# One branch block, forward and backward: stores issued by GpSimd, Z transposed with a later query tile, the last merge transposed by TensorE, x summed in place

## The chip, the cores and the metric

The kernel runs on one core of one Trainium2 chip. The metric is the device time of one execution in microseconds (us), as the median over several runs. TensorE (PE) multiplies, VectorE (DVE), ScalarE (ACT) and GpSimd (POOL) work on its results, and SyncE (SP) does nothing but issue DMAs here: plain copies and DMA transposes.

## The reference

```python
B, T, D, K = 2, 4000, 144, 5                    # all bf16
xa = layernorm(x)
q, k, v = split(xa @ w_qkv)                     # D columns each
p = softmax(q @ k.T * D ** -0.5)                # 4000 x 4000 per batch
glob = (p @ v) @ w_att_out
h = gelu(xa @ w_mlp_in); u, g = split(h)
gc = depthwise_conv(layernorm(g), dw_csgu)      # 5 taps over tokens
loc = (u * gc) @ w_mlp_out
m = concat(glob, loc)
m = m + depthwise_conv(m, dw_merge)             # 5 taps over tokens
out = x + m @ w_merge
...
_out, _vjp = jax.vjp(_f, x, w_qkv, ..., w_merge)
return out, *_vjp(grad_out)                     # out, dx and seven weight gradients
```

## The kernel before

The 4000 tokens of a batch are 32 blocks of 125 rows (`PB`), 64 query tiles for the two batches. Four stages follow each other: a head (loads, layernorms, the weights multiplied together), the attention (`phase_att`, 65 steps, tile i's work spread over several steps), the merge (class `Merge`) and the weight gradients (class `Final`), whose pieces lie between those of the merge.

**A step of the attention.** TensorE makes four pairs of chunks, scores of tile s and dP of tile s-1, each of 1000 columns (128 rows of the contraction in L1181, the 16 left over in L1188). DVE negates a chunk of scores to `Pbuf` and takes its minimum (L1203), ACT exponentiates (L1209) and copies dP to `Sbuf` (L1219), DVE multiplies the two (L1220). SP transposes halves of `Pbuf` and `Sbuf` by DMA to `PT` (L1213) and `ST` (L1408). From these TensorE makes Y (L1230) and Z (L1269), both into one PSUM tile `yz`, of which there is one buffer. Of Y, ACT makes `yn` (L1243, two buffers; stored to `Yn_d`) and three products, and POOL adds two of them to `QBs` (L1252, five buffers). Of Z, DVE makes `zn` (L1273, two buffers; stored to `Zn_d`), which a DMA transpose of its own turns into `zt` (L1281). `X_group` (L1325) sums dS and P against `QBs`, and `zt` against a product of weights, into `acc`. The next query tile, laid out in `qb` of 512 columns, is turned into `qt` by a DMA transpose (L1162).

**Beside it** run the units of the local branch (`local_units`): a group of two blocks passes gelu, layernorm, five taps and their backward; its product `ug` is stored to `ug_d` (L658). Batch 1's layernorm and products (`prep_late`) start at step 27.

**The merge** reads `Yn_d`, `ug_d` and `Zn_d` back (`Yg`, `Zn`), makes transposed copies `goT` and `YT` of 36 blocks, and multiplies them with prepared weights: `out_g` (16 groups of four blocks) forms `po` in PSUM (L1717, L1719), DVE adds it to the loaded `xo` (five buffers) into a tile `o_` (two buffers, L1720), and SP stores `o_`. `dx_a` and `dx_b` make the other output, `dxo`, whose last sum POOL does (L1746) and SP stores. The two batches get their transposed copies in two ways: batch 0 by 72 TensorE transposes and ACT copies (`transposes`, L1529 and L1530), batch 1 by `turn`: POOL copies four blocks to `ym` (L1671, three buffers) and SP issues a DMA transpose (L1672).

**What sets the order.** A `Planner` holds a table of numbers (`ORDER`), one permutation for each engine, and chains the instructions of each engine in that order. Each engine, SP and POOL too, does its list strictly in order: an instruction that waits holds all behind it. `move` (L47, L48) copies 125 rows as 112 and 13. Each DMA also signals one of eight semaphores of its queue in rotation, and waits for the DMA that used that semaphore before it.

Of the kernel before, what the change touches and what calls it, by code (L numbers as in the profile page):

```python
# [8 lines left out]
BF = mybir.dt.bfloat16  # L9
# [6 lines left out]
D = 144  # L16
DR = 16
# [98 lines left out]
class Head:  # L116
# [7 lines left out]
    def loads(self):  # L124
# [287 lines left out]
def prep_late(k, W, b, S, es, pst):  # L412
# [85 lines left out]
    def xar(g):  # L498
# [4 lines left out]
        for c in (2 * g, 2 * g + 1):  # L503
            nc.sync.dma_start(S.XR[32 * (c % 4):32 * (c % 4) + DR, (c // 4) * CH:(c // 4 + 1) * CH], S.R[96:112, c * CH:(c + 1) * CH])
# [17 lines left out]
def local_units(k, W, b, S, A, es, DHT, ps_w, gw):  # L522
# [10 lines left out]
    nc.sync.dma_start(held[1][PB - 1:PB].rearrange("p a b c -> p (a b c)"), k.zdram[0:1, 0:4 * D])  # L533
# [81 lines left out]
    def e_dgc(g):  # L615
# [37 lines left out]
    def gc_unit(g):  # L653
# [4 lines left out]
        nc.sync.dma_start(S.ug_d[:, G2 * g:G2 * g + G2, :], ug[:])  # L658
# [113 lines left out]
class Planner:  # L772

    ORDER = {
# [322 lines left out]
def phase_att(k, W, SS, A, head, E0, E1, prep, hooks):  # L1097
# [30 lines left out]
    def clr():  # L1128
        for t_ in qbr:
            nc.gpsimd.memset(t_[:], 0.0)  # L1130
# [1076 lines left out]
```

## Time and profile before

| | us |
|---|---|
| median of three runs | 1181.19 (1180.3 to 1187.23) |
| profiled execution | 1190.94 |
| its span | 1189.2, granted clock 0.992 |
| busy PE | 1134.5 (95% of the span) |
| busy DVE | 1021.0 (86%) |
| busy ACT | 913.0 (77%) |
| busy POOL | 228.1 (19%) |
| share of the DMA engines' span taken by the hardware queue | 81.4% |

The profiled execution is one single execution, some ten us above the median of the runs beside it; a sum made from its rows is set against its own time. The span runs from the first to the last instruction. Busy times of different engines overlap. The DMA row is the time of the packets on the 16 DMA engines as a share of 16 times the span.

### The profile page before, as it was taken

What the parts mean: (1) busy time and instruction counts of PE and PEld (TensorE: products, weight loads), DVE (VectorE), ACT (ScalarE), POOL (GpSimd) and SP (SyncE); (2) the same over time, 40 slices, a digit from 0 to 9 for tenths busy, and PEclk for the clock granted to TensorE, in tenths of its full rate; (3) what the DMA queues carried; (4) which work ended last, traced back from release to release, by engine and by line L of the source; (5) the groups of instructions that cost most, each with busy time, mean ns of one, the idle gap of its engine ahead of it and who ended that gap; (6) DMA issues with size and microseconds to landing.
All of it is one profiled execution on the core that took longest, in us unless ns stands there. A gap on an engine that the chain in (4) does not pass through costs nothing. (4 is left out here: it accounts for less than half of the span.)

```text
span 1189.2 us, 36104 instructions
## 1 busy us (share of the span) xinstructions
PE 1134.5 (95%) x14389; PEld 880.8 (74%) x14389; DVE 1021.0 (86%) x3043; ACT 913.0 (77%) x1662; POOL 228.1 (19%) x383
## 2 busy tenths in 40 slices
PE   6999999999999889999999999999999999998898
PEld 3667777777777667777676777777777776898887
DVE  8579999999999989778799999999999985676555
ACT  5999888888998766678898888888889766453252
POOL 7111112111112123200011111111111020023441
PEclk9999999999999999999999999999999999999989
DMA  3778888899898999778998988878989889857643
GB/s 106 165 167 167 160 165 176 177 159 182 167 185 165 166 172 203 167 149 170 205 193 160 160 171 161 185 157 172 167 175 165 174 167 181 205 148 185 157 124 97
DMA packets 673144, 198.43 MB, mean 167 GB/s; under 512 B 648915, under 2 KB 666889, under 8 KB 672955
## 3 DMA queue, kind: packets, MB, share of 16 engines
q1 hardware_dynamic: 671846, 194.74, 81.4%
q8 instruction: 112, 1.84, 0.7%
q0 software_dynamic: 592, 1.18, 0.4%
q14 instruction: 56, 0.46, 0.1%
q10 hardware_dynamic: 538, 0.21, 0.1%
HBM read 24.45 MB, written 17.85 MB: 36 GB/s over the span
## 5 line engine op out<-in xcount | busy, mean ns | idle before, releaser
L1203 DVE TENSOR_SCALAR_CACHE_REDUCE Pbuf<-ps 125x1000 bf16<-125x1000 f32 x256 | 306.3, 1197 | 47.0 <-PE ps L1188 37.5
L1219 ACT CAST Sbuf<-ps 125x1000 bf16<-125x1000 f32 x252 | 252.3, 1001 | 101.5 <-PE ps L1188 81.7
L1209 ACT ACTIVATE Pbuf<-Pbuf,nm 125x1000 bf16<-125x1000 bf16 x256 | 284.9, 1148 | 7.7 <-DVE nm L1205 7.4
L1325 PE MATMUL X<-QBs,Sbuf 125*128 125x144 bf16 x2048 | 282.8, 226 | 0.8 <-ACT QBs L1248 0.4
L1325 PE MATMUL X<-QBs,Pbuf 125*128 125x144 bf16 x2048 | 281.5, 226 | 1.0 <-POOL QBs L1252 0.6
L1181 PE MATMUL ps<-xaT_m,qt 128*128 128x500 bf16 x1024 | 262.3, 376 | 6.7 <-DVE Pbuf L1203 4.9
L1325 PEld LDWEIGHTS <-Sbuf 125*128 125x128 bf16 x2048 | 198.4, 98 | 18.7 <-issue 18.3
L1325 PEld LDWEIGHTS <-Pbuf 125*128 125x128 bf16 x2048 | 200.1, 98 | 2.1 <-issue 1.6
L1220 DVE TENSOR_TENSOR Sbuf<-Sbuf,Pbuf 125x1024 bf16<-125x1024 bf16 x252 | 172.0, 687 | 8.0 <-ACT Pbuf L1209 5.4
L1230 PE MATMUL yz<-xa_aug,PT 125*128 125x145 bf16 x2048 | 151.1, 228 | 14.1 <-DMA PT<-Pbuf 13.2
L1269 PE MATMUL yz<-xa_aug,ST 125*128 125x144 bf16 x2048 | 151.4, 229 | 4.9 <-DMA ST<-Sbuf 4.6
L1230 PEld LDWEIGHTS <-PT 125*128 125x128 bf16 x2048 | 131.7, 98 | 29.4 <-DMA PT<-Pbuf 18.7
L1181 PEld LDWEIGHTS <-qt 128*128 128x128 bf16 x1024 | 92.0, 98 | 70.6 <-issue 9.6
L1269 PEld LDWEIGHTS <-ST 125*128 125x128 bf16 x2048 | 133.2, 98 | 14.7 <-issue 8.0
L1252 POOL TENSOR_TENSOR QBs<-g,g 125x144 bf16<-125x144 f32 x64 | 35.7, 558 | 451.1 <-ACT g L1251 293.9
L1332 DVE TENSOR_TENSOR acc<-X,acc 125x432 f32<-125x432 f32 (+1 forms) x204 | 110.1, 547 | 13.7 <-PE X L1325 13.0
L1188 PEld LDWEIGHTS <-qt 16*128 16x128 bf16 x1024 | 26.4, 91 | 110.2 <-issue 110.2
L1188 PE MATMUL ps<-XR,qt 16*128 16x500 bf16 x1016 | 100.4, 380 | 0.0
L1744 ACT ACTIVATE t<-t,dx_c,rstd_x 125x144 f32<-125x144 f32 x64 | 28.6, 500 | 50.7 <-DVE t L1743 45.6
L649 DVE TENSOR_TENSOR l_prod<-ring,Wc 125x720 bf16<-125x720 bf16 x128 | 66.0, 535 | 0.2
L677 POOL TENSOR_SCALAR l_w<-ring,nc,c 125x144 f32<-125x144 bf16 x64 | 30.7, 485 | 176.1 <-DVE nc L673 86.1
L1614 PE MATMUL Hps<-Yg,go_h 125*128 125x144 bf16 x640 | 55.9, 229 | 1.5 <-DMA Yg<-ug_d 1.5
(558 smaller groups left out, 1941.7 us busy)
## 6 DMA issues: line engine op xcount, KB each, us to landing
Yn_d<-yn SPq DMA_DIRECT2D x64, 35.2 KB
Zn_d<-zn SPq DMA_DIRECT2D x64, 35.2 KB
ug_d<-ugr SPq DMA_DIRECT2D x32, 70.3 KB
PT<-Pbuf SPq DMA_TRANSPOSE x126
ST<-Sbuf SPq DMA_TRANSPOSE x126
acc_d<-acc SPq DMA_DIRECT2D x4, 504.0 KB
go_h<-in_grad_out_dram SPq DMA_DIRECT2D x8, 252.0 KB
Yg<-ug_d SPq DMA_DIRECT2D x8, 252.0 KB
```

What stands on the lines that cost most here:

```text
L649: nc.vector.tensor_tensor(prod[:, bi].rearrange("p a b -> p (a b)"), ring[:, a, p + bi:p + bi + 5, :].rearrange("p a b -> p (a b)"), W.Wc[ ...
L1181: mm = nc.tensor.matmul(pp[r // 2][:, r % 2, 0:CH], QT[i][:, 2 * h, :], bs(i)[0].xaT_m[:, c * CH:(c + 1) * CH], start=True, stop=False)
L1188: nc.tensor.matmul(pp[r // 2][:, r % 2, 0:CH], QT[i][rs, 2 * h + 1, :], xr, start=False, stop=True)
L1203: nc.vector.tensor_scalar(pv(pc(i, c2)), src, -1.0, 3.0e38, op0=ALU.mult, op1=ALU.min, accum_out=NM[i][:, c2:c2 + 1])
L1209: nc.scalar.activation(v, v, ACT.Exp, bias=NM[i][:, 4:5], scale=-1.0)
L1219: nc.scalar.copy(pv(sc(i, c2)), src)
L1220: nc.vector.tensor_tensor(sc(i, c2), sc(i, c2), pc(i, c2), op=ALU.mult)
L1230: nc.tensor.matmul(Yw, PT[0:PB, pos(i, j), :], S.xa_aug[:, j, 0:D + 1], start=(j == 0), stop=(j == NB - 1))
L1269: nc.tensor.matmul(Zw, ST[0:PB, j, :], S.xa_aug[:, j, 0:D], start=(j == 0), stop=(j == NB - 1))
L1325: nc.tensor.matmul(X[:, jj, :], l, r, start=(n_ == 0), stop=(n_ == len(ops) - 1))
L1332: nc.vector.tensor_tensor(av, X[0:PB, 0:nj, :], av, op=ALU.add)
L1614: nc.tensor.matmul(H[0:rows, a // 3, (a % 3) * D:(a % 3 + 1) * D], lhs, self.src[b][h][:, 2 + j, :], start=(n == 0 and a % 3 == 0), stop=( ...
```

## The change

Six things are changed together.

1. **Stores by GpSimd.** The stores of `yn` (64), `zn` (64), `ug` (32), `dxo` (32 DMAs) and of batch 0's `xa` (32 DMAs before, 16 after) go from SP's queue to POOL's, with twelve small copies and fills of `prep_late` and `local_units`.
2. **Z with a later query.** `zn` no longer has a tile of its own: it lies in columns 512 to 767 of the query tile `qb`, and the transpose of query tile i turns six blocks in place of four, the last two of them Z of tile i-4. Sixty of the 62 transposes of `zt` are gone, and `qt` has five buffers.
3. **The last merge by TensorE.** `turn` and `ym` are gone: 18 POOL copies and 18 DMA transposes. Batch 1 uses `transposes`, as batch 0 does: 72 TensorE transposes and ten ACT copies.
4. **x summed in place.** `o_` is gone; DVE adds `po` into `xo`, which is stored. `xo` has nine buffers in place of five.
5. **Small things.** Five loads of weights in the head go from ACT's queue to SP's; copies of 125 or 124 rows between `ring`, `held` and `keep` are cut into 112 rows and the rest; nine fills with zeros become two; three columns of statistics share one tile.
6. **A new table** for all five engines. The change's title says that its order was found with the eight DMA semaphores.

```diff
@@ in several places: another queue
-        nc.sync.dma_start(S.Yn_d[:, j0, :], yn[:])
+        nc.gpsimd.dma_start(S.Yn_d[:, j0, :], yn[:])
-        nc.sync.dma_start(S.Zn_d[:, i % NB, :], zn[0:PB, 0:D])
+        nc.gpsimd.dma_start(S.Zn_d[:, i % NB, :], zn[0:PB, 0:D])
-        nc.sync.dma_start(S.ug_d[:, G2 * g:G2 * g + G2, :], ug[:])
+        nc.gpsimd.dma_start(S.ug_d[:, G2 * g:G2 * g + G2, :], ug[:])
-    k.spill_xa0 = lambda j: move(nc.sync, k.xa_d[:, j:j + 2, :], SS[0].xa_aug[:, j:j + 2, 0:D])
+    k.spill_xa0 = lambda j: nc.gpsimd.dma_start(k.xa_d[:, j:j + 2, :], SS[0].xa_aug[:, j:j + 2, 0:D])
-        move(nc.sync, tok_view(k.out1, b)[:, bs, :], dxo)
+        move(nc.gpsimd, tok_view(k.out1, b)[:, bs, :], dxo)
-        ld(self.Wo, k.w_att_out, 0)
-        nc.scalar.dma_start(self.dwt[:], k.dw_merge)
-        ld(self.Wl, k.w_mlp_out, 0)
+        ld(self.Wo, k.w_att_out, 0, nc.sync)
+        nc.sync.dma_start(self.dwt[:], k.dw_merge)
+        ld(self.Wl, k.w_mlp_out, 0, nc.sync)
@@ phase_att
-    qbr = [ab.tile([128, 512], BF, name="qb%d" % i) for i in range(3)]
-    znr = [ab.tile([128, 256], BF, name="zn%d" % i) for i in range(2)]
+    qbr = [ab.tile([128, 768], BF, name="qb%d" % i) for i in range(3)]
+    def zrow(i):
+        return qbr[(i + 4) % 3][:, 512:768]
     def jit_tr(i):
-        QT[i] = gw.tile([128, 4, 128], BF, tag="qt", name="qt")
+        QT[i] = gw.tile([128, 6, 128], BF, tag="qt", name="qt", bufs=5)
         nc.sync.dma_start_transpose(out=QT[i][:], in_=qbr[i % 3][:])
+        if i >= 4:
+            ZN.pop(i - 4)
+            ZT[(i - 4) // NB][(i - 4) % NB] = QT[i][:, 4:6, :]
-        if ok(s - 3):
+        if s - 3 >= NT - 4:
             zt_tr(s - 3)
@@ Merge
-    def turn(self, b, h, j0, n):
-        ...
-        nc.gpsimd.tensor_copy(t[0:PB, 0:n, :], self.src[b][h][:, j0:j0 + n, 0:128])
-        nc.sync.dma_start_transpose(out=self.YT[h][:, j0:j0 + n, :], in_=t[:, 0:n, :].rearrange("p a b -> p (a b)"))
-                out.append(lambda h=h, j0=j0, n=n: self.turn(b, h, j0, n) if b else transposes(k, W, self.src[b][h], self.YT[h], j0, n))
+                out.append(lambda h=h, j0=j0, n=n: transposes(k, W, self.src[b][h], self.YT[h], j0, n))
-        xo = self.wk.tile([PB, GB, D], BF, tag="xo", bufs=5)
+        xo = self.wk.tile([PB, GB, D], BF, tag="xo", bufs=9)
-        o_ = self.wk.tile([PB, GB, D], BF, tag="o_")
-            nc.vector.tensor_tensor(o_[:, 2 * p2:2 * p2 + 2, :], po[:], xo[:, 2 * p2:2 * p2 + 2, :], op=ALU.add)
-        move(nc.sync, tok_view(k.out0, b)[:, b0:b0 + GB, :], o_)
+            nc.vector.tensor_tensor(xo[:, 2 * p2:2 * p2 + 2, :], po[:], xo[:, 2 * p2:2 * p2 + 2, :], op=ALU.add)
+        move(nc.sync, tok_view(k.out0, b)[:, b0:b0 + GB, :], xo)
```

The order of the instructions on three queues shows what this does. **SP in the attention**, before, in batch 1 (the row of `ug_d` is the local branch's store, `qb1` and `qb2` are query tiles):

```order
L1281 DMA_TRANSPOSE zt_17195<-zn0_133 128x2x128
L1213 DMA_TRANSPOSE PT_128<-Pbuf_126 128x16x128
L1408 DMA_TRANSPOSE ST_129<-Sbuf_127 128x16x128
L1244 DMA Yn_d1_73<-yn_17166 125x144
L658 DMA ug_d1_74<-ugr0_10401 125x288
L1162 DMA_TRANSPOSE qt_17397<-qb1_131 128x4x128
```

And after the change, in batch 0, between two query tiles (`dhT` belongs to the local branch):

```order
L1162 DMA_TRANSPOSE qt_13615<-qb1_129 128x6x128
L692 DMA_TRANSPOSE dhT_13457<-dhr0_10235 128x6x128
L1409 DMA_TRANSPOSE ST_127<-Sbuf_125 128x16x128 x2
L1216 DMA_TRANSPOSE PT_126<-Pbuf_124 128x16x128
L1162 DMA_TRANSPOSE qt_13911<-qb2_130 128x6x128
```

Only transposes are left on SP there; the stores and `zt` are gone from between them.

**POOL in the attention**, before, in batch 0 (`l_w`, `ring` and `A_dwc` belong to the local branch):

```order
L677 TENSOR_SCALAR l_w_963<-ring_927,nc1_6599,c0_6601 125x144
L1252 TENSOR_TENSOR QBs_135<-g0_6523,g1_6524 125x144
L620 COPY ring_927<-ring_927 125x2x288
L1252 TENSOR_TENSOR QBs_135<-g0_6819,g1_6820 125x144
L694 TENSOR_TENSOR A_dwc_80<-l_fl_964,A_dwc_80 128x240
```

And after, at about the same place (`xa_d` takes batch 0's layernorm output):

```order
L1245 DMA Yn_d0_69<-yn_6398 125x144
L663 DMA ug_d0_70<-ugr1_921 125x288
L663 DMA ug_d0_70<-ugr0_920 125x288
L1253 TENSOR_TENSOR QBs_131<-g0_6696,g1_6697 125x144
L1992 DMA xa_d_76<-xa_aug0_114 125x2x144 x2
L1245 DMA Yn_d0_69<-yn_6690 125x144
L601 TENSOR_TENSOR rsr1_932<-ve_6756,mhalf_132 125x2
L682 TENSOR_SCALAR l_w_947<-ring_911,nc1_6942,c0_6944 125x144 x2
L1253 TENSOR_TENSOR QBs_131<-g0_7005,g1_7006 125x144
L1275 DMA Zn_d0_71<-qb2_130 125x144
L1275 DMA Zn_d0_71<-qb1_129 125x144
```

The stores now stand between the sums for `QBs`, and some stand a tile or more behind the sum of their own tile (two stores of Z follow each other).

**SP in the merge**, before, a piece in the middle:

```order
L47 DMA out_0_dram<-o__20768 112x576
L48 DMA out_0_dram<-o__20768 13x576
L47 DMA out_0_dram<-o__20709 112x576
L1587 DMA Yg0_20458<-Yn_d1_73 124x288
L1672 DMA_TRANSPOSE YT1_19780<-ym1_19800 128x4x128
L43 DMA Yg0_20458<-Yn_d1_73 13x1152
L1672 DMA_TRANSPOSE goT_92<-ym2_19801 128x4x128
L48 DMA out_0_dram<-o__20709 13x576
L47 DMA out_1_dram<-dxo_21048 112x576
```

And after:

```order
L48 DMA out_0_dram<-xo_19491 13x576
L42 DMA Yg0_20133<-Yn_d1_72 112x1152
L43 DMA Yg1_20136<-ug_d1_73 13x1152
L47 DMA out_0_dram<-xo_19497 112x576
L1588 DMA Yg1_20136<-ug_d1_73 124x288
L48 DMA xo_21492<-in_x_dram 13x576
L47 DMA xa0r_19484<-xa_d_76 112x16x144
```

Before, the stores of `o_` stand behind transposes of `ym`, which wait for POOL's copies; after, no instruction among them waits for POOL, and the stores of `dxo` are gone to POOL's queue.

More of the change, by code (lines that the diff above doesn't have):

```diff
@@ L48, in move, with shift @@
     eng.dma_start(dst[112:PB], src[112:PB])
+def shift(eng, dst, d0, src, s0):
+    for a, n in ((0, 112), (112, PB - 113)):
+        eng.dma_start(dst[d0 + a:d0 + a + n], src[s0 + a:s0 + a + n])
 def halo(k, t, eng):
@@ L1105, in phase_att @@
     ab = es.enter_context(tc.tile_pool(name="att_buf", bufs=1, side="left", reuse_waits="tile"))
-    small = es.enter_context(tc.tile_pool(name="att_small", bufs=4, side="left", reuse_waits="tile"))
     gw = es.enter_context(tc.tile_pool(name="att_gw", bufs=3, side="left", reuse_waits="tile"))
+    small = es.enter_context(tc.tile_pool(name="att_small", bufs=1, side="left", reuse_waits="tile"))
     k.open_batch0()
@@ L1116, in pads @@
         for (buf_, nb_) in ((Pbuf, NPS), (Sbuf, NDS)):
-            for n_ in range(0, nb_, 4):
-                n1 = min(n_ + 4, nb_)
-                nc.sync.dma_start(buf_[PB:128, n_:n1, :].rearrange("p a b -> p (a b)"), k.zdram[0:128 - PB, 0:(n1 - n_) * 1024])
+            nc.sync.dma_start(buf_[PB:128, :, :], k.zdram[0:128 - PB, 0:1024].rearrange("p (a b) -> p a b", a=1).to_broadcast([128 - PB, nb_, 1024]))
             nc.gpsimd.memset(buf_[0:PB, :, :].rearrange("p n (a b) -> p (n a) b", b=128)[:, :, PB:128], 0.0)
@@ L1122, in phase_att @@
     ST = ab.tile([128, NB, 128], BF, name="ST")
-    qbr = [ab.tile([128, 512], BF, name="qb%d" % i) for i in range(3)]
-    znr = [ab.tile([128, 256], BF, name="zn%d" % i) for i in range(2)]
-    QBs = ab.tile([PB, NQB, 2, D], BF, name="QBs")
-    ab.tile([128, 48], BF, name="pad_ab")
+    qbr = [ab.tile([128, 768], BF, name="qb%d" % i) for i in range(3)]
+    QBs = small.tile([PB, NQB, 2, D], BF, name="QBs")
+    k.mhalf = small.tile([128, 48], F32, name="mhalf")
+    nc.vector.memset(k.mhalf[:], -0.5)
     def clr():
         for t_ in qbr:
-            nc.gpsimd.memset(t_[:], 0.0)
-        for t_ in znr:
             nc.gpsimd.memset(t_[:], 0.0)
@@ L1201, in S_min @@
         if c2 == 0:
-            NM[i] = small.tile([PB, 5], F32, tag="nm", name="nm")
+            NM[i] = small.tile([PB, 8], F32, tag="nm", name="nm", bufs=5)
         nc.vector.tensor_scalar(pv(pc(i, c2)), src, -1.0, 3.0e38, op0=ALU.mult, op1=ALU.min, accum_out=NM[i][:, c2:c2 + 1])
@@ L1278, in zt_tr @@
         zn = ZN.pop(i)
-        zt = gw.tile([128, 2, 128], BF, tag="zt", bufs=5)
+        zt = gw.tile([128, 6, 128], BF, tag="qt", name="qt", bufs=5)[:, 4:6, :]
         if i < NT - 2:
-            nc.sync.dma_start_transpose(out=zt[:], in_=zn[:])
+            nc.sync.dma_start_transpose(out=zt, in_=zn)
         else:
@@ L1285, in zt_tr @@
                 nc.tensor.transpose(pt[:, q, :], zn[:, q * 128:(q + 1) * 128], W.ident[:])
-            nc.scalar.copy(zt[:], pt[:, 0:2, :])
+            nc.scalar.copy(zt, pt[:, 0:2, :])
         ZT[i // NB][i % NB] = zt
@@ L1353, in jit_q @@
         rems(i, 0, pj[:, 128:D])
-        QT[i] = gw.tile([128, 4, 128], BF, tag="qt", name="qt")
+        QT[i] = gw.tile([128, 6, 128], BF, tag="qt", name="qt", bufs=5)
         pt = ps_w.tile([128, 4, 128], BF, tag="w")
@@ L1636, in open_late @@
         self.s1, self.s2, self.c0 = ([pm_.tile([PB, NB], F32, name="dx_%s%d" % (n, b)) for b in range(2)] for n in ("s1", "s2", "c0"))
-        self.ym, self.nym = [pm_.tile([128, 4, 128], BF, name="ym%d" % i) for i in range(3)], 0
-        for t in self.ym:
-            k.nc.gpsimd.memset(t[96:128], 0.0)
         self.Zn = [None, None]
@@ L1981 @@
     rstd = [bx.tile([PB, NB], F32, name="rstd_x%d" % b) for b in range(B)]
-    bx.tile([128, 64], BF, name="pad_bx")
     SS = [K() for _ in range(B)]
@@ L2015 @@
     W.ident = k.wpool.tile([128, 128], BF, name="ident")
-    k.mhalf = k.wpool.tile([128, 32], F32, name="mhalf")
     S0 = SS[0]
@@ L2041, in head @@
         pre_load_x(k, 0, S0, [nc.sync])
-        nc.vector.memset(k.mhalf[:], -0.5)
         hd.warm(WARM)
```

66 lines of the change are left out of this document (29 added, 37 removed), and 532 rows, old and new, of the table ORDER.

## The prediction

> **What bounds the kernel now.** I read the view by windows first, because the stages have different limits, with windows cut at the stages' ends: head, attention in three parts, its end with the start of the merge, merge, gradients.
>
> ```profile
> core 0: us, PE busy (x) PEld busy (x) DVE busy (x) ACT busy (x) POOL busy (x), PEclk, DMA share, GB/s
> 30.00:120.00 90.00, 84.86 (x957) 60.53 (x957) 69.13 (x184) 88.78 (x181) 11.12 (x19) 1.00 0.77 165
> 120.00:400.00 280.00, 277.28 (x3494) 210.16 (x3492) 272.01 (x813) 247.20 (x443) 46.16 (x70) 1.00 0.89 170
> 400.00:640.00 240.00, 226.47 (x2807) 171.69 (x2803) 197.68 (x553) 183.71 (x319) 38.50 (x67) 0.99 0.89 177
> 640.00:1000.00 360.00, 355.89 (x4488) 268.95 (x4487) 338.13 (x978) 301.56 (x525) 57.06 (x92) 1.00 0.88 169
> 1000.00:1076.00 76.00, 73.45 (x1086) 67.49 (x1085) 53.17 (x174) 37.95 (x56) 14.65 (x31) 0.98 0.79 187
> 1076.00:1140.00 64.00, 51.36 (x769) 50.67 (x767) 38.52 (x142) 19.43 (x44) 24.78 (x38) 0.92 0.64 148
> 1140.00:1190.00 50.00, 44.65 (x661) 39.80 (x658) 27.30 (x114) 17.68 (x56) 13.23 (x17) 0.98 0.44 114
> ```
>
> The columns are each engine's busy time. From 120 to 400 and 640 to 1000 PE is busy 99% of the time and DVE 97% and 94%: what leaves only SP there buys nothing. From 30 to 120 ACT is full, 88.78 of 90. PE stands still in two places: 13.5 us (240 less 226.47) from 400 to 640, and, more in so short a stretch, 12.6 us (64 less 51.36) from 1076 to 1140, where no engine is full and the clock falls to 0.92. That is the merge, so I asked next what PE waits for from 1000 us on: microseconds in all, times, longest.
>
> ```profile
> PE pm L1538 <- DVE o__20883 L1720: 4.7, 1, 4.7
> PE po L1717 <- DVE o__20650 L1720: 3.1, 1, 3.1
> PE po L1717 <- DVE o__20526 L1720: 2.8, 1, 2.8
> PE yz L1230 <- DMA PT<-Pbuf: 2.3, 1, 2.3
> PE Hps L1614 <- DMA Yg<-ug_d: 1.5, 1, 1.5
> PE po L1717 <- DVE o__20768 L1720: 0.5, 1, 0.5
> ```
>
> Four of the six waits are for DVE's sum of `po` and x. The same sum from DVE's side, for 1076 to 1140, with what DVE was doing in the longest, and PE's clock around two of the waits:
>
> ```profile
> DVE t L1743 <- POOL dxo L1746: 5.0, 3, 2.3
> DVE o__20650 L1720 <- issue: 5.0, 1, 5.0
> DVE o__20828 L1720 <- DMA out_dram<-o__20768: 3.9, 1, 3.9
> ...
> L1720 DVEq EVENT_SEMAPHORE  x30: 21/50/7033, 1070.7 to 1185.2; - x30
> ...
> 1126.41 4.39 DVE L1743 SCALAR_TENSOR_TENSOR t<-xa0r,dx_s,acc 125x144 f32<-125x144 bf16 x3 [1.52 <-POOL dxo L1746]
> ...
> 1102.00:1106.00 4.00, 3.40 (x32) 3.39 (x32) 3.68 (x14) 1.20 (x3) 0.55 (x1) 0.57 1.03 247
> 1130.00:1134.00 4.00, 1.91 (x18) 1.91 (x18) 4.00 (x18) 1.54 (x3) 1.82 (x6) 0.50 0.35 84
> 1134.00:1138.00 4.00, 4.00 (x50) 4.00 (x48) 1.20 (x3) 1.69 (x4) 1.04 (x2) 0.71 0.43 90
> ```
>
> DVE waits up to 7.03 us before it may write `o_`: the buffer's store has not landed, and it could not start, since on SP it stands behind transposes of `ym` that wait for POOL's copies. DVE holds `po`'s buffer meanwhile, and PE stops. The last wait, 4.7 us, is half another thing: three `t` take 4.39 us while POOL makes `dxo` and `ym`. After the stops PE runs at a granted clock of 0.57, 0.50 and 0.71.
>
> **The change part by part**, against the profiled 1190.94 us.
>
> *x in place, and `ym` gone.* Without `o_` the sum waits only for x to be loaded, some groups earlier, nine buffers deep. Saved at most 4.7 + 3.1 + 2.8 + 0.5 = 11.1 us of PE's waits. I count them whole: the mechanism of three is the store of `o_`, and of the 4.7 POOL's copies are gone too. With them goes the slow clock, if PE no longer stops: 3.40 x 0.43 + 1.91 x 0.50 + 4.00 x 0.29 = 3.6 us. Bounds: nothing saved, to 14.7.
>
> *72 transposes on PE*, priced by batch 0's own:
>
> ```profile
> L1529 PE MATMUL pm<-ident,Yg 125*128 125x125 bf16 x72 | 5.4, 218 | 0.0
> L1530 ACT COPY goT<-pm 128x1000 bf16<-128x1000 bf16 (+1 forms) x5 | 4.5, 909 | 3.3 <-PE pm L1529 3.3
> L1530 ACT COPY YT<-pm 128x1000 bf16<-128x1000 bf16 (+1 forms) x5 | 4.5, 906 | 0.4 <-PE pm L1529 0.4
> L1671 POOL COPY ym<-Yg 125x512 bf16<-125x512 bf16 x18 | 11.4, 644 | 30.1 <-DMA goT<-ym 13.4 <-DMA YT<-ym 8.6 <-DMA Yg<-ug_d 3.7
> ```
>
> PE pays 5.4 us, all on the path if nothing stands still there any more. The ten ACT copies, 9.0 us, are hidden: ACT is busy 19.43 + 17.68 of 114 us. POOL loses 11.4 us. Merge: -11.1 - 3.6 + 5.4 = -9.3 us.
>
> *SP's queue in the attention.* SP's cost of an issue, median in the middle:
>
> ```profile
> L1244 SPq DMA_DIRECT2D Yn_d<-yn x64: 250/440/544, 60.2 to 1047.7; - x64
> L1274 SPq DMA_DIRECT2D Zn_d<-zn x64: 250/463/514, 74.6 to 1048.5; - x64
> L658 SPq DMA_DIRECT2D ug_d<-ugr x32: 267/410/497, 125.1 to 989.5; - x32
> L1281 SPq DMA_TRANSPOSE zt<-zn x62: 1167/1224/2427, 73.3 to 1025.2; - x62
> ...
> PE yz L1230 <- DMA PT<-Pbuf: 13.2, 16, 2.9
> PE yz L1269 <- DMA ST<-Sbuf: 4.6, 4, 2.3
> PE ps L1181 <- DMA qt<-qb: 0.9, 2, 0.7
> ```
>
> 64 x 0.44 + 64 x 0.46 + 32 x 0.41 + 60 x 1.22 = 144 us less of issuing, 2.3 us a step (63 steps from 60.2 to 1047.7 us are 15.7 us each). What it can give is bounded by PE's waits for a transpose in the whole run: 13.2 + 4.6 + 0.9 = 18.7 us. The transposes that are left wait mostly for their data, and the larger transpose of `qt` moves half as much again. So I take a quarter, -4.7; bounds -18.7, and above nothing what POOL's queue can cost.
>
> The Trainium skill ("DMA: Bandwidth & Descriptors", section "Why a DMA increments its semaphore by 16 and not by 1") says that a store from SP runs on the largest number of engines up to 16 that divides its rows, five for 125, while one from GpSimd may use all 16; by it the stores would hold the transposes up less than before, nearer to the bound of 18.7 than my quarter, and no row above shows it.
>
> *The stores on POOL.* The DMAs that POOL issues now, its sums for `QBs`, what it waits for, and ACT's wait before `yn`:
>
> ```profile
> L71 POOL DMA_DIRECT2D R<-sWr_d x2: 637/714/791, 667.2 to 699.9; - x2
> L71 POOL DMA_DIRECT2D VUT<-sWm_d x1: 548/548/548, 1036.0 to 1036.0; - x1
> DMA to landing us min/median/max: 3.2/3.9/7.1
> ...
> L1252 POOL TENSOR_TENSOR QBs<-g,g x64: 481/492/995, 50.3 to 1043.8; 125x144 bf16<-125x144 f32 x64
> POOL QBs L1252 <- ACT g L1251: 293.9, 42, 16.1
> PE X L1325 <- POOL QBs L1252: 0.6, 1, 0.6
> L1243 ACTq EVENT_SEMAPHORE  x39: 17/408/2152, 80.5 to 1041.4; - x39
> ```
>
> A DMA holds POOL for 0.55 to 0.79 us. A step brings one store of Y, one of Z, half a `ug` and in batch 0 half an `xa`: three, 1.6 to 2.4 us, on an engine that was busy 46.16 of 280 us, 2.6 us a step. POOL has the time, and PE waited for `QBs` once, 0.6 us. What is queued behind a waiting store is the next `QBs` and the local branch's `l_w`; who waits for those is PE's X. A late store of Y also keeps one of two `yn`, so ACT's next `yn`, so the one PSUM buffer of Y and Z. I take nothing; the upper bound is a rival below. `dxo`'s 32 DMAs, 18 to 25 us, stand where POOL was busy 38 of 114 us and lost 11.4: hidden.
>
> *Head and small things.* Five loads leave ACT, full from 30 to 120; at 0.25 to 0.54 us an issue that is up to 2 us if they stand in that stretch, and the cut copies are as many issues of 0.4 us more on SP. I take nothing, bounds -2 to +2 us. The new table is costed only by its effects above.
>
> Sum: -9.3 - 4.7 = -14.0, so 1176.9 on the profiled execution. That one lies 9.75 us above the median of its runs, so the **forecast is 1167 us** (1181.19 less 14.0), with its own range 1158 to 1175. A change of 1%, 11.8 us, is about what a measurement of this kernel can tell from none.
>
> **The rivals.**
>
> *The transposes come early throughout.* If the waits for `PT`, `ST` and `qt` go whole, the sum is -9.3 - 18.7 = -28.0: 1153 us. For it: 2.3 us a step leave SP, the DMA share falls nowhere below 0.88 in the attention, and 400 to 640 has 13.5 us of idle PE. Against it: the waits are 22 in 63 steps, and the elements that feed the transposes, DVE and ACT, are themselves 97% and 88% busy.
>
> *The waits of the merge change their name.* Batch 1's transposes now take PSUM buffers and ACT's copies between PE's own steps (batch 0's row shows 3.3 us of ACT idle on PE), and `t` still waits for POOL's `dxo`, 5.0 us, whose stores now queue there. If 7 of the 11.1 us come back in this way and the attention gives nothing, -9.3 + 7 = -2.3: 1179 us. For it: 4.39 us for three `t`. Against it: POOL's copies were half of that collision.
>
> *POOL's queue stops the attention.* The stores wait in order on POOL, and one that stands ahead of its data holds `QBs`, one that stands late holds `yn`, then Y's PSUM. At 0.22 us a step the gain of 14.0 is gone (14.0 / 63), from 0.41 us the kernel is slower by over 1%; with 0.5 us, less than one POOL DMA, it is 1167 + 31.5 = 1198 us. For it: ACT waits before `yn` for up to 2.15 us already, PE and DVE have 1 to 6% left, and in the new order stores of a tile lie behind the sum of the next. Against it: POOL waited 293.9 us for ACT at `QBs` alone, so most stores will find it idle.
>
> *DVE holds POOL's DMAs up.* If a store could not be issued while certain operations of DVE run, POOL would stand for about one such operation at each, and two stores ahead of a `QBs` delay it twice. The row that bounds it is 0.79 us against 0.55, so 0.24 us more for one; four times as much, on two stores, a third of it reaching PE, is 0.6 us a step or 40 us: 1207.
>
> The Trainium skill ("SBUF — State Buffer", section "SBUF: two separate sides") states such a lock for DMAs issued by GpSimd, and its section "A bandwidth-pool intuition that's wrong (but worth ruling out)" has about 620 ns alone and 3100 beside a copy by DVE. Of the five DMAs on POOL in this trace none took over 0.79 us, so the trace does not bear it out so far.
>
> **How the numbers follow.** Chances: forecast 0.42, early transposes 0.23, waits renamed 0.18, POOL's queue 0.14, DVE's hold 0.03. That the order does not do what is said can be left out, since the new order shows it. Faster by over 1% (below 1169.4) is the second case and 0.85 of the first: 0.59. Within 1% is the rest of the first and the third: 0.24. Slower is the last two: 0.17. The range leaves out those 0.17 and 0.03 below: from 1146, the second case with half of the 13.5 idle us from 400 to 640 besides, to 1189, where nothing is saved and the 5.4 us of the transposes and 2 us of the head are paid (1181.19 + 7.4).
>
> **What would show it.** Right: from 1076 us on no wait of PE for L1720's successor above 1 us, a clock near 1.0, PE's transposes 5.4 us more and PE busy over 90% there; waits for `PT` and `ST` below 18.7 us; POOL's stores at 0.5 to 0.8 us each; the time between the first and the last `yn` at or under 15.7 us a step. Wrong: the step longer than that, with ACT `yn` or PE's X waiting for POOL or its DMAs; `t` waiting over 5 us for POOL; or the merge as long as before, waiting for loads or ACT.

## The result and the profile after

The changed kernel takes 1191.18 us (median of 20 runs, 1187.42 to 1197.46), the kernel before 1183.13 beside it (20 runs): a ratio of **1.0074 [1.0057, 1.0091]**. It is slower by 0.7%, 24 us above the forecast of 1167 and 2 us above the upper end of the range. Its profiled execution took 1187.62 us, with a span of 1185.8.

The view by windows of the kernel after, cut as it was for the kernel before, with the columns in the same order (each engine's busy time, granted clock, DMA share, GB/s):

```profile
0.00:30.00 30.00, 19.02 (x125) 12.80 (x125) 21.30 (x88) 13.78 (x36) 20.82 (x43) 0.83 0.37 90
30.00:120.00 90.00, 83.54 (x895) 57.08 (x893) 66.23 (x173) 85.49 (x178) 19.33 (x32) 1.00 0.79 159
120.00:400.00 280.00, 271.30 (x3418) 205.89 (x3417) 264.79 (x785) 240.81 (x431) 79.03 (x124) 1.00 0.85 166
400.00:640.00 240.00, 231.47 (x2886) 174.98 (x2885) 202.77 (x568) 191.34 (x330) 68.75 (x118) 1.00 0.95 183
640.00:1000.00 360.00, 354.50 (x4458) 267.37 (x4456) 343.83 (x998) 302.09 (x528) 92.45 (x156) 1.00 0.86 169
1076.00:1140.00 64.00, 62.66 (x1032) 61.78 (x1029) 41.65 (x191) 31.45 (x61) 32.46 (x51) 1.00 0.65 174
```

The last row shows the merge repaired: PE is busy 62.66 of 64 us at full clock, where it was 51.36 at 0.92. From 120 to 400 PE is busy 271.30 of 280, where it was 277.28: 6 us less, in the stage that was to gain (a fixed window does not hold quite the same work in both, since the attention starts later now). The granted clock of the first 30 us is 0.83; before, it was 1.00:

```profile
0.00:30.00 30.00, 20.50 (x150) 11.50 (x150) 25.03 (x94) 16.74 (x46) 22.55 (x51) 1.00 0.38 108
```

PE's waits in the whole span, after:

```profile
PE yz L1233 <- DMA PT<-Pbuf: 9.1, 13, 1.9
PE yz L1270 <- DMA ST<-Sbuf: 6.9, 10, 2.3
PE hps L170 <- DMA raw<-in_w_qkv_dram: 6.7, 1, 6.7
PE ps L1184 <- DVE Pbuf L1206: 6.4, 17, 1.1
PE ps L1184 <- ACT qt L1359: 2.3, 1, 2.3
...
PE ps L1184 <- DMA qt<-qb: 1.3, 2, 0.7
```

No wait for DVE's sum of `po` is among them. For `PT`, `ST` and `qt` PE waits 9.1 + 6.9 + 1.3 = 17.3 us, against 18.7 before, and 8.8 + 2.5 + 1.4 = 12.7 in a second execution of the kernel before: the emptied queue has brought no gain here, and these sums differ by 6 us from one execution to the next.

Since stages move against each other I cut the span at events of the program, not at fixed times: batch 0's first minimum of step 2, of step 16 and of step 50, the last `X`, the end. Length of each piece and PE's idle time in it, in us, worked out from the instructions' times in each trace. Two executions of the kernel before show the spread (4 us from step 16 to 50), so single us there mean nothing:

```
                  to step 2     2 to 16      16 to 50     50 to X     X to end
                  long  idle   long  idle   long  idle   long  idle   long  idle
before            52.0   9.6  215.3   5.9  540.7  17.4  246.3   4.6  134.8  17.2
before, again     51.5   9.3  215.3   5.8  536.8  12.9  245.7   5.1  135.0  18.2
after             58.2  12.8  218.5   8.2  537.5  14.9  247.2   6.7  124.4   7.5
```

The merge gave 10.5 us. The head took 6.4 of them back and the first fourteen steps 3.2. This profiled execution lies 3.6 us below the median of its runs, so the trace shows less than the whole loss.

### The profile page after: what moved, and what is told of

Read it like the earlier page. It is cut to its first block, busy times and chain, and to the rows that moved or that the text cites. A ratio compares the mean times of both kernels' runs of the same rounds, so it can differ in the third digit from the quotient of the medians.

```text
span 1185.8 us, 36236 instructions
## 1 busy us (share of the span) xinstructions
PE 1135.6 (96%) x14461; PEld 881.9 (74%) x14461; DVE 1013.9 (86%) x3043; ACT 922.3 (78%) x1672; POOL 342.5 (29%) x580
## 4 chain that ended last, share of the span: by engine, by line
PE 60%; DMA 13%; DVE 11%; ACT 8%; issue 4%; POOL 2%; SPq 1%; ACTq 0%; POOLq 0%; DVEq 0%
PE X L1326 15%; PE ps L1184 12%; PE yz L1233 7%; PE yz L1270 7%; DMA PT<-Pbuf 5%; PE ps L1191 5%; DVE Pbuf L1206 4%; DMA ST<-Sbuf 3%; ACT Pbuf L1212 3%; PE Hps L1615 3%; PE po L1704 3%; DVE Sbuf L1223 1%; ACT Sbuf L1222 1%; PE pd L611 1%; PE pj L1144 1%
## 5 line engine op out<-in xcount | busy, mean ns | idle before, releaser
L1223 DVE TENSOR_TENSOR Sbuf<-Sbuf,Pbuf 125x1024 bf16<-125x1024 bf16 x252 | 174.7, 698 | 7.7 <-ACT Sbuf L1222 6.2
L1270 PEld LDWEIGHTS <-ST 125*128 125x128 bf16 x2048 | 132.8, 98 | 18.5 <-DMA ST<-Sbuf 10.5
```

The source lines that it names most:

```text
L1223: nc.vector.tensor_tensor(sc(i, c2), sc(i, c2), pc(i, c2), op=ALU.mult)
L1270: nc.tensor.matmul(Zw, ST[0:PB, j, :], S.xa_aug[:, j, 0:D], start=(j == 0), stop=(j == NB - 1))
```

## The experiments

Ratios are to the kernel before, run beside each kernel on the same chip, with 95% intervals. The first theory: the merge gains as forecast, and the head and the stores on POOL take it back.

**The merge.** `b_inplace` is before with the sum in place alone; `b_merge` is before with all of the new merge (in place, TensorE transposes, `dxo` by POOL, the merge in the order of the change), its head and attention untouched, and `b_merge2` is the same kernel once more, beside a later run.

```diff
-        xo = self.wk.tile([PB, GB, D], BF, tag="xo", bufs=5)
-        o_ = self.wk.tile([PB, GB, D], BF, tag="o_")
+        xo = self.wk.tile([PB, GB, D], BF, tag="xo", bufs=9)
@@ b_merge also
-    self.turn(b, h, j0, n) if b else transposes(...)
+    transposes(...)
-        move(nc.sync, tok_view(k.out1, b)[:, bs, :], dxo)
+        move(nc.gpsimd, tok_view(k.out1, b)[:, bs, :], dxo)
```

> The kernel before with only x summed in place (no o_, nine xo buffers), its order unchanged; batch 1 is still transposed by DMA. Theory A (the o_ waits are mostly an accident of one execution): 0 to 5 us faster, ratio 0.996 to 1.000. Theory B (they are always there): 8 to 13 us faster, ratio 0.989 to 0.993, and no wait of PE for L1719 (the sum) above 1 us.

> The kernel before with the merge of the change alone: x summed in place with nine buffers, batch 1 transposed by TensorE, dxo stored by POOL, and the merge's instructions in the order of the change; head and attention as before. From the last X of the attention to the end it took 134.8 and 135.0 us in two profiles before, 131.6 with x in place alone, and 124.4 after. Theory M (the merge's gain is real and stands by itself): 124 to 126 us there and the whole at 1173 to 1177 us, ratio 0.989 to 0.994. Rival (most of it comes from how the attention hands over in the new order): 130 to 134 us there, ratio 0.996 to 1.000.

> Before with only the new merge, once more, beside the run above on the same chip: 0.991 to 0.996 if the gain of the merge stands (0.9935 the first time); a ratio above 0.998 would mean that the first was an accident.

Measured: `b_inplace` 0.9983 [0.9963, 1.0002], no difference that can be told; `b_merge` 0.9935 [0.9909, 0.9960]; `b_merge2` 0.9923 [0.9895, 0.9950], 1175.12 against 1183.52 us. PE's waits from 1000 us on, first in `b_inplace`, then in `b_merge`:

```profile
PE po L1716 <- DVE xo L1719: 7.4, 3, 5.0
PE Hps L1614 <- DMA Yg<-Yn_d: 1.2, 1, 1.2
```

```profile
PE yz L1228 <- DMA PT<-Pbuf: 2.1, 1, 2.1
PE pm L1536 <- POOL Yr L1597: 2.1, 1, 2.1
```

Without `o_` but with the DMA transposes of `ym`, PE still waits 7.4 us for the sum, though no store of `o_` is left to wait for. In the longest of these waits, 5.0 us, DVE's list has a `t` ahead of the sum, and this `t` waits 7.2 us for POOL's `dxo`. Nor were the waits of before an accident of one execution: the second execution has 13.3 us of waits of PE for the sum into `o_` from 1000 us on. Only the new merge as a whole ends them; which of its other edits is needed beside the sum in place was not tried. The merge is worth 0.7%, 8 us.

**The head.** In the trace after, PE's rows with an idle time ahead of them, in the first 20 us, and the clock behind the last of them in stretches of 4 us:

```profile
6.67 0.29 PE L170 MATMUL hps<-ident,raw 128*128 128x128 bf16 x1 [6.67 <-DMA raw<-in_w_qkv_dram]
8.60 0.83 PE L204 MATMUL hps<-two 128*128 128x144 bf16 x4 [0.55 <-ACT two L172]
...
18.29 0.85 PE L1184 MATMUL ps<-xaT_m,qt 128*128 128x500 bf16 x2 [2.29 <-ACT qt L1359]
```

```profile
12.00:16.00 4.00, 3.71 (x25) 2.74 (x25) 2.63 (x16) 1.72 (x5) 1.24 (x3) 1.00 0.68 141
16.00:20.00 4.00, 1.72 (x4) 0.24 (x4) 2.90 (x19) 2.49 (x8) 3.44 (x4) 0.81 0.41 89
20.00:24.00 4.00, 4.00 (x27) 2.99 (x27) 2.96 (x10) 2.40 (x7) 3.42 (x6) 0.50 0.00 1
24.00:28.00 4.00, 4.00 (x29) 3.00 (x29) 1.41 (x6) 2.24 (x5) 3.99 (x11) 0.50 0.13 32
```

ACT's copy of the first `qt` stands behind an `xa_aug` (L383) in ACT's new list; PE pauses 2.29 us and then works for 8 us at half clock. `a_wqkv` swaps ACT's first two instructions, the two loads of `w_qkv`, back. `a_head` does that too, puts the copy of `qt` ahead of that `xa_aug`, and puts ten of PE's filling products (`warm`, whose result nobody reads) together right behind the first scores.

```diff
-        "Activation": [1, 0, 4, ... 14, 11, 15, 18, 38, 16, 12,
+        "Activation": [0, 1, 4, ... 14, 15, 16, 11, 18, 38, 12,
-        "PE": [... 11, 53, 12, 45, 13, 46, 14, 15, 47, 16, 54, 17, 48, 18, 49, 19, 50, 20, 51, 21, 52, 55,
+        "PE": [... 11, 53, 12, 13, 14, 15, 16, 17, 18, 19, 20, 21, 45, 46, 47, 54, 48, 49, 50, 51, 52, 55,
```

> The changed kernel with ACT's first two loads swapped back, so that the 128-row load of w_qkv is issued first and does not stand behind the 16-row load that waits for DVE's fill. In the profile after, PE starts at 6.67 us (4.11 before), and the first yn comes 6.0 us later. Theory H (the head's loss hangs on this load): PE starts about 1.3 us sooner, the first yn comes 1 to 6 us sooner, and the kernel takes 1185 to 1190 us, ratio to before 1.002 to 1.006. Rival (the head is late for other reasons, the x loads and the clock): the first yn at 54 to 55 us again and the ratio 1.007.

> The changed kernel with three moves in the head of the table: ACT's two loads of w_qkv swapped back, ACT's copy of the first qt put ahead of the layernorm activation that waits for POOL, and ten of PE's warming products put behind the first scores. In the profile after, PE stands 2.3 us for that copy at 16 us and then has a granted clock of 0.5 until 28 us; before, it never falls below 1.0 there. Theory H (the head loses 5 to 6 us by that pause and the slow clock behind it): the granted clock stays at 1.0 from 16 to 28 us, the third step's first scores come 4 to 6 us sooner than after (58.2 us), and the ratio is 1.002 to 1.004. Rival (the loss is in the loads and DVE's order): 57 to 59 us and 1.006 to 1.008.

Measured: `a_wqkv` 1.0076 [1.0048, 1.0104], nothing: PE starts at 4.40 us in place of 6.67, but its pause for `qt` grows to 2.90 us and the clock from 16 to 32 us is 0.68, as in the trace after. `a_head` 1.0036 [1.0015, 1.0057], about half of the loss back (its interval just touches that of the change). Up to step 2 it takes 54.1 us against 58.2, and its clock from 16 to 32 us is 1.00 against 0.68:

```profile
16.00:32.00 16.00, 13.80 (x115) 7.37 (x114) 13.73 (x44) 12.02 (x30) 15.28 (x32) 1.00 0.25 65
```

**The stores and the order.** `a_sp` is the changed kernel with the stores of `yn`, `zn`, `ug`, `xa` and `dxo` on SP, at the times at which POOL issued them (`xa` in one DMA, where the kernel before cuts it into 112 rows and 13). `b_pool` is before with the first four on POOL, at the times at which SP issued them. `a_oldatt` is the whole changed program with the head and the attention in the order that the trace of before shows. `a_oldsp` is the same with those four stores on SP: of the change it keeps the merge, Z with the later query, and the small things.

```diff
@@ b_pool, a_oldatt: +;  a_sp, a_oldsp: -
-        nc.sync.dma_start(S.Yn_d[:, j0, :], yn[:])
+        nc.gpsimd.dma_start(S.Yn_d[:, j0, :], yn[:])
... the same for Zn_d, ug_d, xa_d
@@ a_oldatt, a_oldsp: ORDER, by the times of before up to the merge
```

> The changed kernel with the stores of yn, zn, ug, xa and dxo issued by SP again, at the times at which POOL issued them in the profile after; PE, DVE, ACT and the rest of POOL keep the order of the change. Theory P (POOL's queue costs the attention its gain): 4 to 12 us faster than the change, ratio to before 0.997 to 1.004. Rival Q (the stores on SP cost the transposes more): slower than the change by 2 to 10 us, ratio 1.009 to 1.016. Rival N (neither queue matters, the table and the head do): ratio 1.006 to 1.009.

> The kernel before with the stores of yn, zn, ug and xa issued by POOL, each at its old time among POOL's instructions; nothing else changed. Theory P (POOL's queue holds up QBs or yn): 2 to 8 us slower, ratio 1.002 to 1.007, with waits of ACT's yn or PE's X on POOL or its DMAs. Rival Q (SP's queue is freed and the transposes land sooner): 2 to 6 us faster, ratio 0.995 to 0.998, PE's waits for PT and ST below 14 us. Rival N: within 1 us, 0.999 to 1.001.

> The changed program whole (stores on POOL, Z in the query's transpose, TensorE's transposes, x in place, split copies), but with the instructions of head and attention in the order in which they started in the profile before; the merge in the order of the change. Theory O (the new table, not the edits, loses the time): head and attention as before, 1049 to 1055 us to the last X, the merge as after, the whole at 1170 to 1178 us, ratio 0.987 to 0.995. Rival S (the edits lose it: Z's rows in a longer transpose, or POOL's queue): ratio 1.002 to 1.010.

> The changed program with the head and the attention in the order of before, as in the run before this one, and now the stores of yn, zn, ug and xa back on SP at the times they had in before; Z still transposed with a later query, merge as in the change. If the stores on POOL are what the attention pays for (0.82% when they were moved alone), the ratio to before falls from 0.9998 to the merge's alone, 0.991 to 0.996. If it is Z transposed with the query that costs, it stays at 0.998 to 1.002. If neither, between the two: 0.996 to 0.998.

Measured: `a_sp` 1.0112 [1.0085, 1.0140], no better than the change and rather worse (the intervals overlap by a hair); `b_pool` 1.0082 [1.0050, 1.0113], a little more than any of its three theories had; `a_oldatt` 0.9998 [0.9974, 1.0021], between its two theories: the edits and the table each lose a part; `a_oldsp` **0.9882 [0.9853, 0.9910]**, 1170.46 us, faster than both kernels and below all its ranges. So Z with the later query does not cost: beside `b_merge2` on the same chip it gives, with the small things, 4.7 us (1175.12 less 1170.46; the two intervals overlap). The stores on POOL cost about 1% in the old order, and the new order three quarters of a per cent more.

**Which stores.** Before with `yn` and `zn` alone on POOL, with `ug` and `xa`, with `ug`, with `xa`; then the changed kernel in its own order with `ug` and `xa` back on SP (`a_ugxa`), and `a_oldatt` with these two back (`a_best`).

```diff
@@ b_xa
-    k.spill_xa0 = lambda j: move(nc.sync, k.xa_d[:, j:j + 2, :], SS[0].xa_aug[:, j:j + 2, 0:D])
+    k.spill_xa0 = lambda j: nc.gpsimd.dma_start(k.xa_d[:, j:j + 2, :], SS[0].xa_aug[:, j:j + 2, 0:D])
@@ a_ugxa, a_best: the reverse, and ug_d back to nc.sync
```

> Before with only the stores of yn and zn on POOL, all instructions at the times of before. If these 128 stores cost (yn and zn come free later, POOL's sums for QBs wait in line behind them), the ratio is 1.005 to 1.010, as with all four kinds (1.0082). If it is the others, 0.998 to 1.002.

> Before with only the stores of ug and xa on POOL. If the 128 stores of yn and zn are what costs, 0.998 to 1.002 here; if the stores of ug and xa are (they fall in batch 0, whose steps lost most in the change), 1.005 to 1.010; if each takes its share by number, 1.002 to 1.004.

> Before with only the 32 stores of ug on POOL. If ug costs (one each two steps, spread over the attention): 1.005 to 1.009. If xa costs: 0.998 to 1.002. If both share: 1.003 to 1.005.

> Before with only the 16 stores of xa on POOL, all in the head and the first steps of batch 0. If xa costs: the head 3 us longer than before's 51.5 to 52.0 and steps 2 to 16 2 us longer than 215.3, the ratio 1.005 to 1.009. If ug costs: 0.998 to 1.002, head unchanged.

> The changed kernel in its own order, with only the stores of ug and xa back on SP, at the times that they had on POOL. If these two are what it loses: 1.0074 less 0.008, so 0.997 to 1.001. If its order costs by itself, whatever queue the stores are on (with all four kinds back it was 1.0112): 1.005 to 1.012.

> The changed program with head and attention in the order of before, yn and zn stored by POOL, ug and xa by SP. By sums of single parts: 0.9882 with all stores on SP, times 0.9967 for yn and zn: 0.985 (0.982 to 0.988). If Z with the later query already took that gain: 0.986 to 0.990. If POOL's stores hurt in this program whichever they are: 0.992 or more.

| | stores on POOL | ratio |
|---|---|---|
| `b_yz` | 64 `yn`, 64 `zn` | 0.9967 [0.9946, 0.9989] |
| `b_ug` | 32 `ug` | 1.0006 [0.9978, 1.0034] |
| `b_xa` | 16 `xa` | **1.0073 [1.0039, 1.0107]** |
| `b_ugxa` | 32 `ug`, 16 `xa` | 1.0083 [1.0055, 1.0111] |
| `a_ugxa` | the change without `ug`, `xa` | 1.0002 [0.9977, 1.0027] |
| `a_best` | old order, `yn`, `zn` | 0.9898 [0.9853, 0.9942] |

Sixteen of these 176 stores do the harm; the others cost nothing that can be told. `a_best` was to be better than `a_oldsp` and is the same within its interval. The stores on POOL in the trace after (ns min/median/max of an issue, first and last start; under each the time to landing):

```profile
L1245 POOL DMA_DIRECT2D Yn_d<-yn x64: 528/546/618, 73.6 to 1050.7; - x64
DMA to landing us min/median/max: 1.7/3.0/6.3
L1275 POOL DMA_DIRECT2D Zn_d<-qb x64: 528/544/629, 83.2 to 1059.1; - x64
DMA to landing us min/median/max: 1.8/3.0/6.0
L663 POOL DMA_DIRECT2D ug_d<-ugr x32: 528/531/597, 122.2 to 987.4; - x32
...
L1992 POOL DMA_DIRECT2D xa_d<-xa_aug x16: 1179/1213/1416, 35.2 to 531.7; - x16
DMA to landing us min/median/max: 4.0/4.7/7.5
```

A store of `xa` holds POOL for 1.21 us, the others for 0.53 to 0.55. It takes two slots of 144 out of rows of 160, 250 pieces of 288 bytes; the others are 125 pieces, of 288 bytes too for `yn` and `zn`. It is the number of pieces in one store that goes with the harm, not the number in all (the 128 stores of `yn` and `zn` are 16000 pieces, those of `xa` 4000) and not their bytes alone. On SP's queue an issue does not go by pieces: the same 250 in one DMA took 0.46 us there (`a_sp`).

Where that reaches PE shows against `b_ug`, the same order with `xa` on SP. By the first minimum of each step, `b_ugxa` lies 0.2 us behind at step 1, 2.7 at steps 2 to 8, 4.4 at step 9 and 5.3 at step 12: it loses at three places, and at each stores of `xa` have just been issued. From there on the lag moves between 2.9 and 6.3 us and is 4.4 us at the last step; the spans are 1189.0 and 1183.1. PE's waits for `PT` from 30 to 215 us, over these three places, in `b_ugxa`; `b_ug` has none there:

```profile
PE yz L1228 <- DMA PT<-Pbuf: 4.2, 3, 2.0
```

(`b_xa` itself is not used here: its profiled execution took 1183.77 us, 11 us less than the median of its runs, and does not show the loss.) The trace of `b_ugxa` around step 9: PE's wait (from 148 to 164 us), then POOL's and SP's rows:

```profile
PE yz L1228 <- DMA PT<-Pbuf: 1.6, 1, 1.6
```

```profile
152.99 1.25 POOL L2004 DMA_DIRECT2D xa_d<-xa_aug  x1
154.24 0.57 POOL L658 DMA_DIRECT2D ug_d<-ugr  x1
154.80 1.19 POOL L2004 DMA_DIRECT2D xa_d<-xa_aug  x1
...
151.63 6.22 SPq L1211 DMA_TRANSPOSE PT<-Pbuf  x2
```

And `b_ug` there, where PE has no wait:

```profile
148.89 4.91 SPq L1212 DMA_TRANSPOSE PT<-Pbuf  x2
153.86 0.54 SPq L48 DMA_DIRECT2D xa_d<-xa_aug  x1
154.50 4.25 SPq L1407 DMA_TRANSPOSE ST<-Sbuf  x2
```

The two transposes of `PT` take SP 6.22 us beside the stores of `xa`, 4.91 without, and PE waits for `PT`, not for POOL. The group of this line alone gives the second transpose as 3.14 us, against 1.82 at most in `b_ug`:

```profile
L1211 SPq DMA_TRANSPOSE PT<-Pbuf x2: 1542/2342/3143, 151.6 to 154.7; - x2
```

```profile
L1212 SPq DMA_TRANSPOSE PT<-Pbuf x2: 1657/1740/1822, 148.9 to 152.0; - x2
```

One transpose of over 3 us proves little by itself: the kernel before, with no store on POOL, has transposes of `PT` and `ST` of up to 3.78 us. So I compared all of them, the k-th transpose of `PT` or `ST` of one trace with the k-th of another. Of the transposes that overlap a store of `xa` on POOL, from its issue to its landing, the mean in us, and the mean of the same transposes in a trace with the same order of the other work (in `a_ugxa` the stores of `ug` are on SP as well):

| transposes beside a store of `xa` | mean | the same ones in | mean |
|---|---|---|---|
| 19 of `b_ugxa` | 2.24 | `b_ug` | 1.77 |
| 18 of `b_xa` | 2.33 | before | 1.77 |
| 20 of after | 2.64 | `a_ugxa` | 2.04 |

Half a microsecond on each, 9 to 12 us in all. The other transposes of `b_ugxa` up to 540 us take 1.84 against 1.88 in `b_ug`, so the difference lies beside these stores. Beside the stores of `yn` and `zn`, 101 transposes of `b_yz` take 2.06 against 1.98 in before: 0.1 us.

**The pieces.** The last pair keeps `xa` on POOL and stores its rows whole, 160 wide: 125 pieces of 640 bytes, half the pieces with 11% more bytes (the first expectation below says 14%; 640 against 576 are 11%). One is made from `b_xa`, one from the changed kernel in its own order.

```diff
-    k.xa_d = tc.dram_tile([PB, NB, D], BF, name="xa_d")
+    k.xa_d = tc.dram_tile([PB, NB, XW], BF, name="xa_d")
-        nc.gpsimd.dma_start(k.xa_d[:, j:j + 2, :], SS[0].xa_aug[:, j:j + 2, 0:D])
+        nc.gpsimd.dma_start(k.xa_d[:, j:j + 2, :], SS[0].xa_aug[:, j:j + 2, :])
-        nc.gpsimd.memset(S.xa_aug[:, :, D:D + 1], 1.0)
+        nc.gpsimd.memset(S.xa_aug[:, :, D:XW], 1.0)
```

> Before with the 16 stores of xa on POOL, as in b_xa, but whole rows of 160 instead of 144, so that each partition is one piece of 640 bytes (125 pieces for a store, not 250; 14% more bytes). If the number of pieces is what holds POOL and the transposes beside it up, an issue falls from 1.21 us to about 0.57, SP's transposes beside it to the usual 1.7 us, and the ratio from 1.0073 to 0.998 to 1.003. If it is xa on POOL's queue as such, or its bytes, 1.005 to 1.010 as before.

> The changed kernel, all its stores on POOL and its own order, with the same cut of xa into 125 pieces of 640 bytes. If the pieces are the cause, the ratio falls from 1.0074 to 0.999 to 1.004; if not, it stays at 1.005 to 1.010.

Measured: `a_xa145` **1.0003 [0.9978, 1.0028]**, against 1.0074; `b_xa145` 1.0025 [0.9993, 1.0057], against 1.0073. An issue of `xa` in `a_xa145`:

```profile
L1992 POOL DMA_DIRECT2D xa_d<-xa_aug x16: 530/536/767, 31.8 to 523.4; - x16
DMA to landing us min/median/max: 1.9/3.3/5.8
```

Same queue, same order, more bytes: 1.21 us fall to 0.54, the landing from 4.7 to 3.3, and the kernel's loss is gone. In this pair only the changed kernel tells clearly; for `b_xa` the two intervals overlap, though most of its loss is back. The 18 transposes that take 2.33 us in `b_xa` take 1.84 in `b_xa145`. In the changed kernel less of this is seen: its 20 fall from 2.64 to 2.41 us, so there the way from the pieces to the 0.7% is not fully shown. One place is visible in it from 370 to 392 us, where two stores of `xa` are issued at 370.6 and 371.8 us (in `a_xa145` at 364.3 and 364.8). PE's wait there, after, then in `a_xa145`:

```profile
PE yz L1270 <- DMA ST<-Sbuf: 2.3, 1, 2.3
```

```profile
PE yz L1270 <- DMA ST<-Sbuf: 0.4, 1, 0.4
```

## Why the prediction was wrong, step by step

Laid end to end, the runs account for the result (the ratios were measured on different chips, so each step is uncertain by 0.3 to 0.5%):

| added | kernel | ratio | step |
|---|---|---|---|
| the merge | `b_merge2` | 0.9923 | -0.8% |
| Z with the later query, small things | `a_oldsp` | 0.9882 | -0.4% |
| `yn`, `zn` on POOL | `a_best` | 0.9898 | none to be told |
| `xa`, `ug` on POOL | `a_oldatt` | 0.9998 | +1.0% |
| the new order of head and attention | after | 1.0074 | +0.8% |

*x in place, and `ym` gone: right.* The forecast was -9.3 us. `b_merge` and `b_merge2` give 0.65% and 0.77%, 8 to 9 us, and the stage is 10.5 us shorter. PE's waits, the clock and the 62.66 of 64 us came as said. One detail was off: "without `o_` the sum waits only for x to be loaded". The sum in place alone, which was given most of the 11.1 us, is not enough (`b_inplace`), because DVE does the sum behind a `t` that waits for POOL.

*SP's queue: the size agrees, but by luck.* -4.7 us was forecast, a quarter of a bound, and `a_oldsp` against `b_merge2` gives 4.7, with some 3 us of uncertainty in each. In `a_oldsp` the stores still stand on SP: the gain comes with the folded transposes, about half of the 144 us that were to leave SP, and the small things. Moving the stores of `yn` and `zn` off SP gives 0.3% in the kernel before (`b_yz`) and nothing that can be told in `a_best`. In the changed kernel the waits for transposes stay at 17.3 us, in `a_best` they are 2.7 + 0.9 + 2.8 = 6.4 from 55 to 1045 us:

```profile
PE ps L1184 <- DMA qt<-qb: 2.8, 1, 2.8
PE yz L1233 <- DMA PT<-Pbuf: 2.7, 7, 0.8
...
PE yz L1270 <- DMA ST<-Sbuf: 0.9, 1, 0.9
```

So the rival of the early transposes was half right under the old order: the waits fall by 6 to 12 us against the two executions of before. But `a_best` gains 12 us in all, 8 to 9 of them in the merge, so 3 to 4 us of these waits came back as time, not 18.7.

*The stores on POOL: this is the first step that failed.* "I take nothing" holds for `yn`, `zn` and `ug`. It fails for `xa`, which the text counted as "half an `xa`" a step at 0.55 to 0.79 us like the rest. Its shape, 125x2x144 out of rows of 160, stood in the order that was quoted. The price was taken from DMAs of POOL that all have one piece per row (the trace before has fifteen of them, 0.50 to 0.79 us, not five); that of `xa` is 1.21 us. Worse, the cost was looked for in POOL's own queue, and it lies on another: SP's transposes beside such a store take half a microsecond longer. In place of nothing, the 16 stores cost 0.7% (`b_xa`), 8 to 9 us; cut into 125 pieces, `xa` costs nothing that can be told (`a_xa145`). That the pieces are the cause is shown in the changed kernel. That they act through the transposes is what `b_ugxa` shows, where PE's waits for `PT` make 4.2 of the 5.3 us lost by step 12; in the changed kernel one place shows it, but there the slower transposes get back only part of their time without the 250 pieces. Why a transpose is slowed by them was not tried.

The Trainium skill ("Perfetto Trace Analysis", section "DMA Instruction — SWDGE (GPSIMD)") says that such an instruction of GpSimd ends in the profile when its last descriptor is written. This case's trace agrees: the interval of an `xa` is 1.21 us and its landing comes at 4.7, and half the pieces make it 0.54 us.

*"The new table is costed only by its effects above": this is the second.* The order alone costs 0.8% between `a_oldatt` and after, and 1.0% between `a_best` and `a_ugxa`, where `xa` is on SP in both. The term *head and small things*, taken as 0 with bounds of 2 us, had the place but not the cause: not five loads, but ACT's copy of `qt` and PE's pause (in the old order one of the five, `dwt`, does make PE wait, 1.8 to 2.2 us in `a_oldsp`, `a_oldatt` and `a_best`). `a_head` gives 0.4% of it back. The other half lies in the attention: from the first minimum of step 16 to the last `X`, five traces of the changed program in the new order (after, `a_wqkv`, `a_head`, `a_ugxa`, `a_xa145`) take 782.2 to 791.1 us, three in the old order (`a_oldatt`, `a_oldsp`, `a_best`) 775.7 to 781.4. Which instructions of the new order cost it is open. Queue and order also act together: in the new order all the stores on SP give 1.0112 (`a_sp`), and with `yn`, `zn` and `dxo` on POOL 1.0002 (`a_ugxa`, where `xa` goes in two DMAs), while in the old order the queue of `yn` and `zn` makes 0.3% at most.

*The rivals.* "The waits of the merge change their name" is right in its place and harmless: DVE's wait for `dxo` grows from 5.0 to 17.9 us, which the forecast had named as a sign of being wrong, and PE has none from it:

```profile
DVE t L1730 <- POOL dxo L1733: 17.9, 7, 4.3
```

"POOL's queue stops the attention" named 1198 us and came nearest in time, but not in its mechanism: PE waits 0.4 us for `QBs`, ACT 0.6 us for a store of Y before `yn`, and from the first `yn` to the last a step takes 15.78 us, where the same rows before give 15.75. "DVE holds POOL's DMAs up" is not seen: 160 stores beside a busy DVE took 0.53 to 0.63 us, and the 1.21 us of `xa` went with its pieces. The 3100 ns that the Trainium skill has for a DMA of GpSimd beside a copy by DVE ("SBUF — State Buffer", section "A bandwidth-pool intuition that's wrong (but worth ruling out)") appear nowhere here.

## What to carry to other kernels

Price a DMA that GpSimd issues by the number of pieces it is cut into, and not by its bytes: before a store goes to GpSimd, make each partition's part contiguous, even if that stores padding too. Look for its cost on the other queues as well, at what is in flight beside it. And an order that was made anew is a change of its own: put the old order under the new program once, since here it took the loss of 0.7% away, and with `xa` and `ug` back on SP left a gain of 1.0 to 1.2%.

## What had not been expected of the hardware

Beside a store of 250 pieces from POOL, SP's transposes of 16 blocks take 2.24 us in the mean (`b_ugxa`), the same ones 1.77 without it (`b_ug`). And a pause of PE of only 2.29 us was followed by a clock of 0.50 for 8 us; in `a_xa145` a pause of 2.25 us at the same place was followed by a mean of 0.89 from 16 to 32 us, against 0.68, and in `a_ugxa` one of 2.18 us by 1.00, so the price of such a pause is not the same each time. The row of the pause in `a_xa145`, then the clock after, in `a_xa145` and in `a_ugxa`:

```profile
17.80 0.60 PE L1184 MATMUL ps<-xaT_m,qt 128*128 128x500 bf16 x2 [2.25 <-ACT qt L1359]
```

```profile
16.00:32.00 16.00, 13.71 (x86) 8.43 (x86) 10.55 (x37) 9.96 (x26) 12.56 (x26) 0.68 0.16 37
16.00:32.00 16.00, 14.09 (x112) 8.36 (x113) 13.61 (x44) 12.07 (x31) 14.47 (x32) 0.89 0.23 56
16.00:32.00 16.00, 13.70 (x98) 7.50 (x97) 11.97 (x41) 10.52 (x29) 13.29 (x27) 1.00 0.20 52
```
